# Token blocks of 512 with one u buffer, heads computed from row halves, first loads as two heads side by side

## The chip, the cores and the metric

One core of one Trainium2 chip runs the kernel. The metric is the device time of one execution in microseconds (us); a comparison uses the median of several runs.

## The reference

A batch of 8 sequences goes through attention and then through a feed-forward part. Cut to what matters:

```python
# q, k, v: (8 batches, 8 heads, 576 positions, 64); U (576, 32), V (32, 576)
# w_ch1 (512, 2048), w_ch2 (2048, 512)
scores = (q @ k.transpose(0, 1, 3, 2)) / 8
local   = (rel >= 0) & (rel < 32)                       # heads 0 to 3
strided = (rel >= 0) & (pos[None] % 32 == pos[:, None] % 32)   # heads 4 to 7
attn = softmax(np.where(mask, scores, -1e9))
x = (attn @ v).transpose(0, 2, 1, 3).reshape(8, 576, 512)
u = x + (x.transpose(0, 2, 1) @ U @ V).transpose(0, 2, 1)      # mixing over positions
out = u + np.maximum(u @ w_ch1, 0) @ w_ch2                     # on each token alone
```

U, V and both weight matrices arrive as 64-bit floats; the kernel makes each into two 32-bit parts, high and low.

## The kernel before

**Two halves of the work.** The feed-forward part is two chains of matmuls on TensorE. `gemm1(n, fc)` computes 128 of the 2048 hidden columns (`fc` from 0 to 15) for token block `n`: 12 matmuls into one PSUM bank `ph`, 4 slices of the 512 input columns times 3 products of high and low parts. ACT then makes `gh` (relu, rounded) and DVE makes `gl` (the rest). `gemm2` multiplies `gh` and `gl` with the second weights and adds into `acc`. A block has 256 tokens (two tiles of 128), so there are 18 blocks and 288 steps, each of 12 matmuls of 256 columns (`gemm1`, line 625) and 6 of 512 columns (`gemm2`, line 642). Blocks 0 and 1 are run interleaved (`NLEAD`), because the weights are still being converted then.

**Attention beside it.** Batches 0 and 1 (`attention_pair` with `early`) work on pairs of heads: TensorE transposes q and k (`transpose_natural`, line 203), ACT copies the result out in four pieces for each of q and k (lines 204 to 213), k into `kZ`, a buffer that holds the two heads on its diagonal and zeros elsewhere, so that one matmul of 128 rows does both heads (line 299, 18 of them, each in two passes). The strided heads of these batches use the same code on values that a DMA has reordered in DRAM (`sd`) and pass their result through DRAM (`od`). The local heads of batches 2 to 7 take q and k transposed by DVE (lines 287, 289); their strided heads (`strided_heads`) are products on GpSimd (lines 409, 437) and sums on DVE (lines 411, 439). `mix_t` and `mix_u` do the mixing over positions (lines 475, 479, 501, 508).

**The token transposes.** `transposes(n)` prepares `uh` and `ul`, the transposed block in two parts: on TensorE for three blocks (line 590), later by DVE and 16 DMAs. These live in a ring of 5 buffers with tag `u`, so the next block's parts can be written while this block's are read.

**What sets the order.** The Python loop at the end emits the steps of all of these side by side by a table of numbers at the top of the file; a scheduler then fixes the order of instructions on each engine, and each engine works in that order. Nearly all DMAs are issued by SP's queue. Weight chunks (32 of 512 KB) are loaded by line 157 and converted by `to_f32` and `weights` on ACT, DVE and GpSimd.

Of the kernel before, what the change touches and what calls it, by code (L numbers as in the profile page):

```python
# [7 lines left out]
F32 = mybir.dt.float32  # L8
# [9 lines left out]
ATT_BUFS = 7  # L18
NSP = 2
N_STEPS_1 = 90  # L20
N_LOCAL = 60
N_STRIDED = 66
LAG = 2
LAGB = 5
DUPS = 'aaaaaaaadapaaada'
EVK = 'aaaaaaaaaaaaaaaa'
EVQ = 'vaaaaaaaaaavaaaa'
PTS = 'vaaaaaaa'
CMODE = (1, 1, 1, 0, 1, 1, 1, 0)
W0, W1 = 2, 29  # L30
N_PE_T = 3
LD0, LDR = 4, 0.3
LDM = 4
CONVM = 1.35
NLEAD = 2
SKEW = 2
CLA = 2
SW0 = 2
SD_N = 1
S_END = 16  # L40
CONV0, CONV1, CONVE = 6, 99, 5
B1S, B1E = 24, 1
ORDER0, ORDER1 = (0, 2, 3, 1), (0, 2, 3, 1)
# [3 lines left out]
def fused_kernel(ctx, tc, q, k, v, U, V, w1_in, w2_in, masks, eye, out):  # L47
# [8 lines left out]
    FPG = NFC // NG  # L56

# [15 lines left out]
    def ubuf(shape, name, dtype=F32):  # L73
        return mp.tile(shape, dtype, name=name, tag="u", bufs=5)

    counts = {"xn": 0, "conv": 0}
    banks = {"n": 0, "prefix": True}

    def psx2():
        """Two PSUM banks; those of the output sums serve too before the first of them."""  # L80
        banks["n"] += 1
        if banks["prefix"] and banks["n"] % 3 == 0:
            return ps_acc.tile([128, 2, 512], F32, name="acc")
        return ps_x.tile([128, 2, 512], F32, name="px")
# [8 lines left out]
    def dma(out, in_):  # L93
        last_dma[0] = nc.sync.dma_start(out=out, in_=in_).ins  # L94

    ident = const.tile([128, 128], F32, name="ident")
    masks_sb = const.tile([128, 768], BF16, name="masks_sb")
    mask_b = masks_sb[:, 0:640].rearrange("p (a t x) -> p a t x", a=2, x=64)
    ident_b = masks_sb[:, 640:768]
    kZ = const.tile([128, 2, 32 + S], F32, name="kZ")  # L100
    nc.vector.memset(kZ, 0.0)
# [4 lines left out]
    def to_f32(raw, p, n, eng=nc.vector, one=False):  # L106
# [3 lines left out]
        cv = att([128, 512], "cv")  # L110
        f = cv[0:p, 0:n]
        if one:
            eng.tensor_scalar(out=f, in0=hi_w.bitcast(F32), scalar1=TINY, scalar2=None, op0=ALU.abs_max)
        else:
            nc.scalar.activation(out=f, in_=hi_w.bitcast(F32), func=AF.Abs)  # L115
# [669 lines left out]
```

## Time and profile before

| what | number |
|---|---|
| runs | 1017.5 us median, 1016.81 to 1020.14 |
| profiled execution: span from first to last instruction | 1016.9 us |
| TensorE matmul busy | 958.7 us (94%) |
| VectorE (DVE) busy | 648.8 us (64%) |
| ScalarE (ACT) busy | 313.0 us (31%) |
| GpSimd (POOL) busy | 406.1 us (40%) |
| first matmul of `gemm1` starts at | 90.94 us |

The profiled execution lies 0.6 us below the median of the runs. The page's chain of work that ended last puts 76% of the span on TensorE. The text calls the time before the first `gemm1` the opening, the time in which blocks 0 and 1 run the first 512 tokens.

### The profile page before, as it was taken

What the parts mean: (1) busy time and instruction counts of PE and PEld (TensorE: products, weight loads), DVE (VectorE), ACT (ScalarE), POOL (GpSimd) and SP (SyncE); (2) the same over time, 40 slices, a digit from 0 to 9 for tenths busy, and PEclk for the clock granted to TensorE, in tenths of its full rate; (3) what the DMA queues carried; (4) which work ended last, traced back from release to release, by engine and by line L of the source; (5) the groups of instructions that cost most, each with busy time, mean ns of one, the idle gap of its engine ahead of it and who ended that gap; (6) DMA issues with size and microseconds to landing.
All of it is one profiled execution on the core that took longest, in us unless ns stands there. A gap on an engine that the chain in (4) does not pass through costs nothing.

```text
span 1016.9 us, 18249 instructions
## 1 busy us (share of the span) xinstructions
PE 958.7 (94%) x7164; PEld 832.6 (82%) x7164; DVE 648.8 (64%) x1184; ACT 313.0 (31%) x691; POOL 406.1 (40%) x397
## 2 busy tenths in 40 slices
PE   4576889999999999999999999999999999999997
PEld 2345678898898889978889888988898889999996
DVE  3567998979786868634768686968686864312121
ACT  6777545213311241111422133123321242111110
POOL 1324966965383429201447353735383410000000
PEclk9797999999999999999999999999999999999999
DMA  7865913042523250401252425052514200101000
GB/s 189 221 164 143 366 39 67 2 109 48 91 42 68 48 90 22 88 1 42 47 91 43 68 47 91 21 89 48 91 39 71 47 22 21 42 1 43 1 21 21
DMA packets 186094, 71.33 MB, mean 70 GB/s; under 512 B 148952, under 2 KB 177272, under 8 KB 186008
## 3 DMA queue, kind: packets, MB, share of 16 engines
q1 hardware_dynamic: 186008, 70.16, 32.4%
q8 instruction: 56, 0.92, 0.4%
q14 instruction: 30, 0.25, 0.1%
HBM read 51.64 MB, written 11.80 MB: 62 GB/s over the span
## 4 chain that ended last, share of the span: by engine, by line
PE 76%; DVE 7%; SPq 5%; POOL 4%; issue 3%; DMA 3%; ACT 2%; DVEq 0%; POOLq 0%; ACTq 0%
PE ph L625 35%; PE acc L642 33%; SPq L94 4%; POOL tmp L409 3%; PE px L299 2%; PE px L340 1%; DVE cv L120 1%; DVE st L439 1%; PE px L330 1%; POOL w L170 1%; SPq L157 1%; DVE cv L122 1%; PE px L475 1%; DMA raw<-in_moe_w_ch_dram 1%; PE px L501 1%
## 5 line engine op out<-in xcount | busy, mean ns | idle before, releaser
L625 PE MATMUL ph<-uh,w 128*128 128x256 f32 x2304 | 472.6, 286 | 8.1 <-DVE gl L630 7.3
L625 PEld LDWEIGHTS ph<-uh,w 128*128 128x128 f32 x2304 | 379.3, 190 | 29.4 <-DVE gl L630 11.9
L642 PE MATMUL acc<-w,gh 128*128 128x512 f32 x1088 | 341.5, 393 | 0.0
L625 PE MATMUL ph<-ul,w 128*128 128x256 f32 x1152 | 331.5, 288 | 1.6 <-DVE ul L595 1.6
L630 DVE SCALAR_TENSOR_TENSOR gl<-ph,gh 128x256 fp32r<-128x256 f32 x288 | 120.6, 419 | 244.9 <-ACT gh L629 243.5
L629 ACT ACTIVATE gh<-ph 128x256 fp32r<-128x256 f32 x288 | 110.3, 384 | 504.9 <-PE ph L625 452.8
L437 POOL TENSOR_TENSOR tmp<-st,s_st 128x448 f32<-128x448 f32 (+7 forms) x162 | 144.2, 912 | 237.2 <-DVE st L439 148.7
L625 PEld LDWEIGHTS ph<-ul,w 128*128 128x128 f32 x1152 | 217.3, 189 | 11.4 <-DVE ul L595 1.8
L642 PEld LDWEIGHTS acc<-w,gh 128*128 128x128 f32 x1088 | 194.3, 188 | 31.2 <-issue 2.2
L642 PE MATMUL acc<-w,gl 128*128 128x512 f32 x544 | 213.2, 392 | 0.2 <-DVE gl L630 0.2
L409 POOL TENSOR_TENSOR tmp<-st 128x576 f32<-128x576 f32 (+6 forms) x162 | 169.4, 1089 | 74.9 <-DMA st<-in_k_dram 29.2
L439 DVE TENSOR_REDUCE st<-tmp 128x64 f32<-128x64 f32 (+8 forms) x162 | 138.3, 873 | 4.4 <-POOL tmp L437 3.4
L642 PEld LDWEIGHTS acc<-w,gl 128*128 128x128 f32 x544 | 102.2, 188 | 19.3 <-issue 1.1
L411 DVE TENSOR_REDUCE s_st<-tmp 128x9 f32<-128x576 f32 (+6 forms) x162 | 87.8, 564 | 14.2 <-POOL tmp L409 13.6
L170 POOL TENSOR_TENSOR w<-cv,w 128x512 fp32r<-128x512 f32 x32 | 45.3, 1424 | 49.1 <-ACT w L169 46.9
L116 POOL TENSOR_SCALAR cv<-cv 128x512 f32<-128x512 f32 x24 | 40.0, 1670 | 42.2 <-ACT cv L115 36.8
L454 ACT COPY xg<-st 32x256 f32<-32x256 f32 x96 | 38.7, 404 | 37.3 <-DVE st L439 36.4
L299 PE MATMUL px<-kZ,qT 128*32 128x128 f32 x612 | 30.5, 303 | 8.5 <-ACT qT L226 8.4
L299 PEld LDWEIGHTS px<-kZ,qT 128*32 128x32 f32 x612 | 20.4, 120 | 18.3 <-ACT qT L226 9.9
L169 ACT CAST w<-cv 128x512 fp32r<-128x512 f32 x32 | 19.7, 618 | 44.0 <-DVE cv L122 37.4
L612 DVE TENSOR_TENSOR ul<-u,uh 128x1024 fp32r<-128x1024 f32 x15 | 21.9, 1460 | 14.3 <-ACT uh L611 14.3
L120 DVE SCALAR_TENSOR_TENSOR cv<-raw,cv 128x512 int32<-128x512 int32 x32 | 28.3, 888 | 0.4
(123 smaller groups left out, 686.6 us busy)
## 6 DMA issues: line engine op xcount, KB each, us to landing
raw<-in_moe_w_ch_dram SPq DMA_DIRECT2D x32, 512.0 KB, 8.0
out_dram<-xg SPq DMA_DIRECT2D x32, 256.0 KB, 2.2
u<-bt SPq DMA_DIRECT2D x240, 32.0 KB, 1.9
vt_kept<-in_v_dram SPq DMA_DIRECT2D x28, 144.0 KB, 3.6
st<-in_q_dram SPq DMA_DIRECT2D x24, 144.0 KB, 3.4
st<-in_k_dram SPq DMA_DIRECT2D x24, 144.0 KB, 4.8
st<-in_v_dram SPq DMA_DIRECT2D x24, 144.0 KB, 3.2
xn<-in_k_dram SPq DMA_DIRECT2D x48, 72.0 KB, 2.4
```

The costliest lines, as they stand in the source:

```text
L94: last_dma[0] = nc.sync.dma_start(out=out, in_=in_).ins
L116: eng.tensor_scalar(out=f, in0=f, scalar1=TINY, scalar2=None, op0=ALU.max)
L170: nc.gpsimd.tensor_tensor(out=lo, in0=f, in1=hi.bitcast(F32), op=ALU.subtract)
L299: nc.tensor.matmul(sp[32 * c4:32 * c4 + 32, t], qT[:, 32 * c:32 * c + 32], kZ[:, :, 32 * c:32 * c + 64], start=not early, stop=True, skip_ ...
L409: nc.gpsimd.tensor_tensor(out=tmp[:, 0:n], in0=sk[:, j0:j0 + n], in1=sq[:, i:i + 1].broadcast_to([128, n, D]), op=ALU.mult)
L411: late.append(lambda tmp=tmp, n=n, i=i, j0=j0: nc.vector.tensor_reduce(out=s_st[:, i, j0:j0 + n], in_=tmp[:, 0:n], axis=AX.X, op=ALU.add))
L437: nc.gpsimd.tensor_tensor(out=tv, in0=sv[:, 0:i + 1, d0:d0 + step], in1=s_st[:, i, 0:i + 1].broadcast_to([128, i + 1, step]), op=ALU.mult)
L439: late.append(lambda tv=tv, i=i, d0=d0, step=step: nc.vector.tensor_reduce(out=o_st[:, i, d0:d0 + step], in_=tv.rearrange("p j d -> p d j" ...
L625: nc.tensor.matmul(ph[:, 0:W], w_parts[0, g, dc][:, part, fs], ut[:, :, :, dc, :], start=(dc == 0 and i == 0), stop=(dc == NDC - 1 and i = ...
L629: nc.scalar.activation(out=gh[:, 0:W], in_=ph[:, 0:W], func=AF.Relu)
L630: nc.vector.scalar_tensor_tensor(out=gl[:, 0:W], in0=ph[:, 0:W], scalar=0.0, in1=gh[:, 0:W].bitcast(F32), op0=ALU.max, op1=ALU.subtract)
L642: nc.tensor.matmul(accs[n][:, s, :], gt[:, cs], w_parts[1, g, f][:, part, :], start=(fc == 0 and i == 0), stop=(fc == NFC - 1 and i == 2))
```

## The change

**Blocks of 512 tokens.** A block is now four tiles of one batch (`blocks`), and a ninth block takes the last 64 positions of all batches. `gemm1` and `gemm2` each issue 12 matmuls of 512 columns, in 144 steps. `acc` takes four PSUM banks, and the banks of the attention go from two buffers of two to one (`ps_x`, `bufs=1`).

**One u buffer.** `transposes(n)` brings the transposed tokens to `raw`; `split(n)` makes the high and low part of all four tiles in the one buffer `u` when the last `gemm1` of the block before has been issued.

**Heads from row halves.** `kZ` goes away. q and k of two heads stand in rows 0 to 63 and 64 to 127 of one buffer, and `scores` and `outputs` issue 36 matmuls of 64 rows each instead of 18 of 128 rows; the two heads write to separate PSUM banks. The mask comes in by two matmuls with an identity in all batches (before, in batches 2 to 7, DVE added it).

**First loads.** `load_natural` loads each head by a DMA of 256-byte pieces (before, 512-byte pieces over both heads), so that one copy of 576 columns follows the transposes. The second copy of the values, which ACT made for most heads of batches 0 and 1, is a DMA (`values`). The first seven DMAs of batch 0 that are not k go to ACT's queue. Batch 1 starts after 10 steps of batch 0 instead of 24 (`B1S`), and a weight chunk is converted every 2 steps instead of every 5 (`CONVE`).

```diff
-    ps_acc = ctx.enter_context(tc.tile_pool(name="ps_acc", bufs=1, space=bass.MemoryType.PSUM))
+    ps_acc = ctx.enter_context(tc.tile_pool(name="ps_acc", bufs=2, space=bass.MemoryType.PSUM))
...
-    ps_x = ctx.enter_context(tc.tile_pool(name="ps_x", bufs=2, space=bass.MemoryType.PSUM))
+    ps_x = ctx.enter_context(tc.tile_pool(name="ps_x", bufs=1, space=bass.MemoryType.PSUM))
...
+    def values(vt, heads, eng=None):
+        for hh in range(2):
+            sv = heads[hh].rearrange("(c p) d -> p c d", p=32)
+            dma(out=vt[64 * hh + 32:64 * hh + 64, :, 0:D], in_=sv, eng=eng)
+            dma(out=vt[64 * hh:64 * hh + 32, 1:NCH, 0:D], in_=sv[:, 0:NCH - 1, :], eng=eng)
...
+    def scores(kT, qT, mask):
+        sp = psx2()
+        for hh in range(2):
+            nc.tensor.matmul(sp[:, hh, 0:320], ident_b, mask, start=True, stop=False, skip_group_check=True)
+        for c in range(NCH):
...
+            for hh, rows in enumerate(halves):
+                nc.tensor.matmul(sp[32 * c4:32 * c4 + 32, hh, x0:64 * t + 64], qT[rows, 32 * c:32 * c + 32],
+                                 kT[rows, k0:32 * c + 32], start=False, stop=True, skip_group_check=True,
+                                 tile_position=(64 * hh, 32 * c4))
...
+    def load_natural(src, h0, eng=None):
...
+        for hh in range(2):
+            dma(out=xn[:, 0:512].rearrange("p (t h d) -> p h t d", h=2, d=D)[:, hh],
+                in_=src[h0 + hh, 0:512].rearrange("(t p) d -> p t d", p=128), eng=eng)
...
+    blocks = [[(xg_b, t) for t in range(4)] for xg_b in range(B)] + [[("T", p) for p in range(B // 2)]]
...
+        uT[n] = mp.tile([128, 2, 4, 4, NDC, 32], F32R, name="u", tag="u", bufs=1)
...
+    def split(n):
+        u, raw = u_tile(n), raw_u[n]
+        for dc in range(NDC):
+            src, hi, lo = raw[:, :, :, dc, :], u[:, 0, :, :, dc, :], u[:, 1, :, :, dc, :]
+            nc.scalar.copy(out=hi, in_=src)
+            nc.vector.tensor_tensor(out=lo, in0=src, in1=hi.bitcast(F32), op=ALU.subtract)
...
-                nc.tensor.matmul(ph[:, 0:W], w_parts[0, g, dc][:, part, fs], ut[:, :, :, dc, :],
+                nc.tensor.matmul(ph, w_parts[0, g, dc][:, part, fs], uT[n][:, ut, :, :, dc, :],
                                  start=(dc == 0 and i == 0), stop=(dc == NDC - 1 and i == 2))
-        gh = mp.tile([128, 256], F32R, name="gh", bufs=3)
-        gl = mp.tile([128, 256], F32R, name="gl", bufs=3)
...
+        gh = mp.tile([128, 512], F32R, name="gh", bufs=2)
+        gl = mp.tile([128, 512], F32R, name="gl", bufs=2)
...
+                    if fc == NFC - 1 and n + 1 < NB:
+                        split(n + 1)
```

Three places show how the order moves. In the rows, `x12` is a count and the sizes are of what is written.

TensorE at a block change (the end of the eighth of 18 blocks before, of the fifth of 9 blocks after; `w_3_3` is the fourth slice of the last quarter of the weights, `w_0_0` the first of the first). Before, the new block's `gemm1` stands between the last `gemm2` of the old block:

```order
L625 MATMUL ph<-uh,w_3_3_1628 128x256
L642 MATMUL acc<-w_3_1_1695,gh 128x512 x2
L642 MATMUL acc<-w_3_1_1695,gl 128x512
L642 MATMUL acc<-w_3_1_1695,gh 128x512 x2
L642 MATMUL acc<-w_3_1_1695,gl 128x512
L625 MATMUL ph<-uh,w_0_0_257 128x256
```

After, ten more `gemm2` matmuls stand behind the old block's last `gemm1`, and then these rows up to the first step of the new block, which reads the new contents of the one buffer `u`:

```order
L604 MATMUL acc<-w_3_2_1785,gh 128x512 x2
L604 MATMUL acc<-w_3_2_1785,gl 128x512
L246 MATMUL px<-vt_84,PT_6177 32x65 x8
L604 MATMUL acc<-w_3_3_1794,gh 128x512 x4
L604 MATMUL acc<-w_3_3_1794,gl 128x512 x2
L246 MATMUL px<-vt_84,PT_6177 32x65 x28
L588 MATMUL ph<-u,w_0_0_231 128x512 x3
L588 MATMUL ph<-u,w_0_1_309 128x512 x3
L588 MATMUL ph<-u,w_0_2_386 128x512 x3
L588 MATMUL ph<-u,w_0_3_503 128x512 x3
```

So 18 `gemm2` matmuls and a head pair's 36 output matmuls stand between the last `gemm1` of the old block and the first of the new; a second step of `gemm1` (12 matmuls), 6 matmuls of `gemm2` and the third step of `gemm1` follow.

DVE at a block change. Before, the low part of the next block (line 612) is one instruction among the strided sums:

```order
L630 SCALAR_TENSOR_TENSOR gl<-ph,gh 128x256
L411 TENSOR_REDUCE s_st<-tmp 128x9
L612 TENSOR_TENSOR ul<-u,uh 128x1024
L411 TENSOR_REDUCE s_st<-tmp 128x7
L630 SCALAR_TENSOR_TENSOR gl<-ph,gh 128x256
```

After, between the last `gl` of a block (line 593) and the first of the next, with the four low parts of `split` (line 578) and the final sums of the old block (line 608):

```order
L593 SCALAR_TENSOR_TENSOR gl<-ph,gh 128x512
L436 TENSOR_REDUCE st<-tmp 128x32
L578 TENSOR_TENSOR u<-raw,u 128x16x32 x2
L436 TENSOR_REDUCE st<-tmp 128x32
L578 TENSOR_TENSOR u<-raw,u 128x16x32 x2
L436 TENSOR_REDUCE st<-tmp 128x32 x2
L608 TENSOR_TENSOR xg<-acc,xg 128x512 x2
L436 TENSOR_REDUCE st<-tmp 128x32
L256 TENSOR_SCALAR rt<-px 128x2x4
L436 TENSOR_REDUCE st<-tmp 128x32 x3
L257 RECIPROCAL rt<-rt 128x2x4
L593 SCALAR_TENSOR_TENSOR gl<-ph,gh 128x512
```

Eight sums, four low parts and two final sums of the old block now stand ahead of the new block's first `gl`.

ACT ahead of the first `gemm1`. Line 553 writes `u` for the four tiles of block 0; all four are needed by its first matmul. Three conversions, whose chunks are loaded after all of batch 1's q and k, stand between them:

```order
L553 CAST u<-acc 128x4x4x32
L227 ACTIVATE s_sb<-s_sb 128x640
L553 CAST u<-acc 128x4x4x32
L99 ACTIVATE cv<-raw_1_3_1150 128x512
L99 ACTIVATE cv<-raw_1_0_1228 128x512
L553 CAST u<-acc 128x4x4x32
L99 ACTIVATE cv<-raw_1_1_1245 128x512
L553 CAST u<-acc 128x4x4x32
```

Before, the same place has the two tiles of block 0 alone, with the first `gemm1` waiting for those two:

```order
L594 CAST uh<-px 128x4x4x32
L169 CAST w_0_2_789<-cv 128x512
L594 CAST uh<-px 128x4x4x32
```

The last write that the first `gemm1` needs now stands behind three more conversions, and so behind their loads.

More of the change, by code (lines that the diff above doesn't have):

```diff
@@ new lines, in fused_kernel, with x_tiles, copy @@
+    halves = [slice(64 * hh, 64 * hh + 64) for hh in range(2)]
+    held = {}
+    vts = []
+    def x_tiles(b):
+        if b not in xgs:
+            xgs[b] = xp.tile([128, 4, DM], F32, name="xg")
+        if b // 2 not in tails:
+            tails[b // 2] = tail("xt")
+        return xgs[b], tails[b // 2]
+    def copy(engine, out, in_):
+        if engine == "a":
+            nc.scalar.copy(out=out, in_=in_)
+        else:
+            (nc.vector if engine == "v" else nc.gpsimd).tensor_copy(out=out, in_=in_)
@@ new lines, in outputs @@
+    def outputs(PT, vt, p0):
+        op = psx2()
+        for c in range(NCH):
+            t, c4 = c // 4, c % 4
+            o4 = c4 + p0 // 32 if t == 4 else c4
+            for hh, rows in enumerate(halves):
+                nc.tensor.matmul(op[32 * o4:32 * o4 + 32, hh, (D + 1) * t:(D + 1) * t + D + 1], PT[rows, 32 * c:32 * c + 32],
+                                 vt[rows, c], start=True, stop=True, skip_group_check=True,
+                                 tile_position=(64 * hh, 32 * o4))
+        return op[:, :, 0:5 * (D + 1)].rearrange("p h (t x) -> p h t x", x=D + 1)
@@ L687, in fused_kernel @@
+    gen, sgen = second(1), None
+    for i, _ in enumerate(first(0)):
+        if i >= SW0:
+            next(sw, None)
+        if i >= CONV0 and i % CONVE == 0:
+            convert(counts["conv"] + 1)
+        if i >= B1S and i % B1E == 0:
+            next(gen, None)
+    u_tile(0)
+    for _ in transposes_pe(0):
+        convert(counts["conv"] + 1)
     banks["prefix"] = False
     pend = []
[L689 to L690 removed]
+    c0 = counts["conv"]
```

725 lines of the change are left out of this document (317 added, 408 removed).

## The prediction

> **What bounds the kernel now.** I read the page's slices of the span first, then the groups of instructions by shape, then the chain of waits. In the slices (busy tenths, 25 us each) TensorE is near full from about 150 us to the end, and only the first six slices leave it room:
>
> ```profile
> PE   4576889999999999999999999999999999999997
> DVE  3567998979786868634768686968686864312121
> PEclk9797999999999999999999999999999999999999
> ```
>
> Its two large groups are the feed-forward matmuls, and the chain says how fast they follow each other when nothing else is there (start, length, what):
>
> ```profile
> L625 PE MATMUL ph<-uh,w 128*128 128x256 f32 x2304 | 472.6, 286 | 8.1 <-DVE gl L630 7.3 <-ACT uh L594 0.7
> L642 PE MATMUL acc<-w,gh 128*128 128x512 f32 x1088 | 341.5, 393 | 0.0
> ...
> 879.44 2.91 PE ph L625 x24
> 882.35 3.17 PE acc L642 x14
> ...
> 924.45 2.91 PE ph L625 x24
> ```
>
> The means of 286 and 393 ns overlap; the pitch is what counts. It is 2.91/24 = 121.25 ns for 256 columns and 3.17/14 = 226.4 ns for 512. Sixteen steps of 12 and 6 make 45.0 us, just the distance from 879.44 to 924.45. All 288 steps cost 288 x (12 x 0.12125 + 6 x 0.2264) = 810.3 us of the 1016.9 us span. The same two lines counted by stretches of the span (busy, then count; line 625 first) give the rest:
>
> ```profile
> 90.90:205.60 114.70, 54.25 (x379) 50.83 (x380) 0.99 0.37 118
> 205.60:880.00 674.40, 348.06 (x2533) 332.68 (x2532) 1.00 0.32 57
> 880.00:1011.60 131.60, 73.08 (x548) 71.50 (x546) 1.00 0.06 19
> ...
> 90.90:205.60 114.70, 47.22 (x176) 30.70 (x176) 0.99 0.37 118
> 205.60:880.00 674.40, 327.15 (x1264) 223.66 (x1264) 1.00 0.32 57
> 880.00:1011.60 131.60, 72.30 (x288) 51.24 (x288) 1.00 0.06 19
> ```
>
> Counts times pitches: in the middle stretch (batches 2 to 7) 593 us are feed-forward and 81.3 us are not, 13.5 us for each batch. In the stretch of the first 512 tokens 85.8 us are feed-forward and 28.9 us are not. The last is pure. So the span is 90.9 (opening) + 114.7 + 674.4 + 131.6 + 5.3 (last sum and store). It lies 0.6 us under the median of the runs, and I add that at the end.
>
> **Part 1: wide gemm1.** The change turns 3456 matmuls of 256 columns into 1728 of 512. At the pitch that `gemm2` has with 512 columns of the same type, each pair saves 2 x 121.25 - 226.4 = 16.1 ns, 27.8 us in all. The bounds: the moving tokens of `gemm1` are read in runs of 32 elements and those of `gemm2` in one run, so at worst the pitch stays in proportion to columns and the gain is 0. I take 27.8: a fixed cost c and a cost per column from the two rows give c = 16 ns, and the 256-column rows are already read in such runs. Nothing can hide this gain, since TensorE is the engine that ends the chain. The Trainium skill, "TensorE: Matmul & The Clock Gate", section "Wait — 56ns, not 53.3ns?", puts the fixed cost of a matmul at about 2.5 ns; by that this part would be an estimated 1728 x 2.5 ns = 4.3 us. The trace does not agree: 226.4 and 121.25 ns stand where the page's sum gives 215.8 and 109.2.
>
> **Part 2: heads from row halves.** Before and after, per pair of heads (start, length of a merged run, what):
>
> ```profile
> 343.18 1.32 PE L340 MATMUL px<-vt_kept,PT 128*32 128x130 f32 x36
> 344.43 0.50 PE L642 MATMUL acc<-w,gl 128*128 128x512 f32 x1
> ...
> 349.70 1.28 PE L299 MATMUL px<-kZ,qT 128*32 128x128 f32 x36
> 350.92 0.43 PE L304 MATMUL px<-kZ,qT 128*64 128x128 f32 x2
> 351.28 0.39 PE L625 MATMUL ph<-uh,w 128*128 128x256 f32 x1
> ...
> 68.05 0.43 PE L479 MATMUL ph<-xt,U_sb 64*32 64x64 f32 x16
> ```
>
> ```profile
> L479 PE MATMUL ph<-xt,U_sb x16: 216/216/240, 68.0 to 68.3; 64*32 64x64 f32 x16
> ```
>
> Scores take 351.28 - 349.70 = 1.58 us, outputs 344.43 - 343.18 = 1.25 us. The shape that replaces them, 64 rows by 32 with 64 columns, is there in line 479: 16 records in 0.43 us, of which the last lasts 0.216, so 15 pitches of 14.3 ns. After, 72 records are 1.03 us. The two mask matmuls (640 columns) cost about 0.38 us, so scores are 1.41 and outputs 1.04: 0.38 less for each of 12 pairs, and 0.05 for a narrower transpose, -5.2 us. The bounds: as fast as that row, or 30 ns, the pitch of today's 128-column records without any gain for half the width (1.22 us / 36 = 34), which would add 22 us instead. I take the row of the same shape.
>
> **Part 3: the opening.** Here the path is a queue of loads, conversions and head pairs before the first `gemm1`:
>
> ```profile
> 90.94 0.50 PE L625 MATMUL ph<-uh,w 128*128 128x256 f32 x2 [0.68 <-ACT uh L594]
> ...
> 76.61 1.10 SPq L94 DMA_DIRECT2D xn<-in_q_dram  x2
> ...
> 46.10:49.00 2.90, 0.00 (x0) 0.00 (x0) 1.67 (x2) 2.83 (x7) 1.15 (x1) 0.69 0.72 216
> 268.00:272.00 4.00, 4.00 (x35) 3.06 (x28) 0.59 (x2) 0.72 (x3) 0.00 (x0) 1.00 1.36 170
> 98.00:108.00 10.00, 9.78 (x62) 8.40 (x62) 8.95 (x15) 6.99 (x15) 8.33 (x6) 0.98 0.95 352
> 0.00:90.90 90.90, 51.09 (x625) 35.86 (x625) 46.30 (x99) 67.32 (x108) 22.85 (x24) 0.85 0.73 184
> ```
>
> The last column is GB/s: 216 where q and k come in 512-byte pieces, 170 where everything comes in 256-byte pieces, 352 where weights come. ACT is the busiest engine of the opening (67.3 of 90.9 us). The change takes 13 copies of values and most of 64 part copies away there:
>
> ```profile
> L226 ACT COPY kZ<-acc 64x288 f32<-64x288 f32 x12 | 8.0, 664 | 1.4 <-PE acc L203 1.2
> L226 ACT COPY vt_kept<-vt_kept 32x1088 f32<-32x1088 f32 x6 | 6.7, 1112 | 0.1
> ```
>
> 13 x 1.11 = 14 us, and about 20 us of the 36 that the part copies take, so ACT no longer sets the pace. The loads do. From the order of SP's queue, ahead of batch 1's last q stand after the change 10.1 MB in 256-byte pieces, 1.5 MB in larger ones and 5.5 MB of weights, masks and U, V: 59.4 + 6.9 + 15.6 = 82 us, against 3.7, 6.0 and 5.5 MB, 22 + 28 + 16 = 65 us, before (where the last q is issued at 76.6 us, so 13 us more went in waits). Behind that q come values (0.6 MB), the `od` round trip and three weight chunks, about 15 us, and ACT's order sets those chunks' conversions ahead of the last write of `u`. With 5 us of waits the first `gemm1` starts at 102 us instead of 90.9: +11 us. Bounds: 87 us, if the conversions hold nothing up, and 115, if the loads wait as much as today.
>
> **Part 4: the first 512 tokens.** TensorE works there for 103.6 of 114.7 us:
>
> ```profile
> 90.90:205.60 114.70, 103.56 (x740) 88.76 (x741) 105.84 (x180) 50.05 (x101) 90.68 (x67) 0.99 0.37 118
> ```
>
> So 11.1 of the 28.9 us are idle and 17.8 are attention and transposes. By the order, after the change all eight pairs' scores and seven of eight outputs of batches 0 and 1 stand ahead of the first `gemm1`; of batch 1 only a transpose (0.65), an output (1.04), two `mix_t` (1.6), `mix_u` (1.15) and their switches (1.3) remain, 5.7 us. The 12 us that move into the opening lie beside its loads (TensorE works 51 of 90.9 us there). DVE, 105.8 of 114.7 us busy, is what TensorE idles for; 14 instead of 7 conversions are done before, so I leave 5 us of idle. 28.9 becomes 10.7: -18.2 us. Bounds: 8 to 22 us left.
>
> **Part 5: block changes.** Now `u` is single, and DVE must do, between the last `gl` of a block and the first of the next, what the excerpt of its order shows:
>
> ```profile
> L439 DVE TENSOR_REDUCE st<-tmp 128x32 f32<-128x576 f32 x12 | 14.2, 1203 | 0.0
> L439 DVE TENSOR_REDUCE st<-tmp 128x32 f32<-128x320 f32 x12 | 8.6, 727 | 0.0
> L649 DVE TENSOR_TENSOR xg<-acc,xg 128x512 f32<-128x512 f32 x30 | 19.4, 683 | 5.6 <-PE acc L642 5.3
> ...
> PE ph L625 <- DVE gl L630: 7.3, 8, 1.5
> ```
>
> Eight sums of about 1.0, six operations of 0.68 (line 649's shape), two small ones and the `gl` itself (0.68): 13.1 us, up to 1.3 less because neighbours overlap. TensorE waits for it at the third `gemm1` step, whose bank the first `gl` must free: 48 matmuls (10.9 us), the outputs (1.25) and switches, 12.5 us after the last `gemm1` of the old block. With relu in front (0.6) DVE is late by 0 to 1.2 us. I take 1 us for each of 8 changes, +8 us; bounds 0 and, if DVE comes late to it, 5 us each, 40 us. Behind this wait stands all of TensorE's queue. In the whole run today TensorE waits 7.3 us for `gl` before `gemm1`. The tail stays: one sum and the stores behind the last matmul.
>
> **Sum.** -27.8 - 5.2 + 11 - 18.2 + 8 = -32.2: 984.7 against the 1016.9 us of the profiled execution, 985 against the median.
>
> **Rivals.**
> - *The opening does not grow.* For it: ACT loses 34 us of work, seven first loads go to another queue. Against it: 10.1 MB at 170 GB/s. With the first `gemm1` at 87 us the time is 970.
> - *Small matmuls pay by record.* For it: today's 128-column records run at 34 ns, no row shows row halves by turns. Against it: 14.3 ns in line 479. At 25 ns, 24 sets of 72 records behind the opening cost 72 x 10.7 ns = 0.77 us each: +18.5, 1003 us. The Trainium skill, same page and section, states that start to start never drops below about 25 ns however small the matmul is; by that rule this would be the case, and the row of line 479 disagrees.
> - *The fixed cost of a matmul is not 16 ns but per column.* Against it: the two pitches. The gain of part 1 is then 0, 1012 us; by the page's 2.5 ns an estimated 1008.
> - *Slower: DVE is late at every block change.* Place: the third `gemm1` step of a block, waiting for the first `gl`. For it: 13.1 us of DVE work against 12.5 of cover, and the steps before it load DVE fully (sums and transposes). Against it: 64% DVE over the span. The sum without part 5 is 976.7, so it decides from 40.8/8 = 5.1 us per change; at 6 us it is 1025.
>
> **How the numbers follow.** The forecast has 0.55, with a range of its own of 968 to 1002; the opening that does not grow 0.20, records 0.11, columns 0.05, DVE late 0.09. The range takes the first three cases with the bounds of parts 3 to 5: 956 to 1012. The bound of a measurable difference is 0.3%, 3 us. All cases but the last are faster, the per-column one just about: faster 0.87, same 0.04, slower 0.09.
>
> **What the profile after would show.** Part 1: 24 matmuls of line 588 or 604 in a row at 226 ns each, 5.43 us a step. Part 2: a run of line 214 or 246 about 1.0 us long. Part 3: first line 588 at about 102 us, ACT's conversion waiting for weights before it. Part 4: first block ended about 98 us later. Part 5: line 588 waiting for `gl` of line 593 about 8 us in all, at eight places. Wrong would be: an opening over 115 us, `gemm1` at 240 ns, or a wait of several us at each change.

## The result and the profile after

The changed kernel takes 1045.3 us (median of 4 runs, 1042.2 to 1047.0) against 1018.1 for the kernel before: a ratio of 1.0262 with a 95% interval of 1.0237 to 1.0286. It is slower by 27 us where 32 us less were forecast, and lies outside the range of 956 to 1012. The profiled execution has a span of 1044.6 us.

The slices of the span (25 us each, busy tenths) show a longer opening at a low clock, and TensorE as the full engine behind it:

```profile
PE   4457798989999999989999999999999999999997
PEclk8566799999999999999999999999999999999999
```

The same three stages of both kernels, first after, then before, cut at the first `gemm1` and at the first `gemm1` of token 512. The columns are length; busy time and count of TensorE, its weight loads, DVE, ACT and POOL; granted clock; DMA share; GB/s:

```profile
0.00:110.49 110.49, 60.61 (x1265) 41.09 (x1265) 60.42 (x123) 46.56 (x74) 29.50 (x32) 0.68 0.94 203
110.49:223.13 112.64, 104.24 (x645) 78.56 (x646) 104.97 (x161) 39.35 (x69) 95.74 (x75) 0.95 0.43 113
223.13:1044.60 821.47, 792.89 (x4960) 614.09 (x4958) 445.24 (x734) 171.42 (x363) 274.98 (x290) 0.99 0.25 47
```

```profile
0.00:90.94 90.94, 51.09 (x625) 35.86 (x626) 46.34 (x99) 67.35 (x109) 22.89 (x24) 0.85 0.73 184
90.94:207.38 116.44, 105.34 (x750) 90.35 (x751) 107.50 (x182) 50.41 (x102) 92.42 (x69) 0.99 0.37 119
207.38:1016.90 809.52, 802.30 (x5790) 706.42 (x5788) 494.96 (x906) 195.22 (x481) 290.74 (x306) 1.00 0.28 50
```

So the opening is 19.6 us longer, the first 512 tokens are 3.8 us shorter, and the rest is 12.0 us longer. In the rest, TensorE is busy 9.4 us less, and stands still 28.6 us instead of 7.2.

The chain that ended last, in undisturbed steps near the end (start, length, what):

```profile
961.36 2.84 PE ph L588 x12
964.20 2.80 PE acc L604 x12
```

`gemm1` follows at 2.84/12 = 237 ns and `gemm2` at 2.80/12 = 233 ns. A step of 24 matmuls takes 5.645 us, where the same work took 2 x 2.813 = 5.63 us before and 5.43 was predicted. The first term of the sum is not there. (Pitches of single matmuls in this text, such as 226.8 ns for the kernel before, are means of the distances between starts in undisturbed steps near the end.)

What TensorE waited for (total, times, longest, in us):

```profile
PE ph L588 <- DVE gl L593: 14.2, 6, 3.0
...
PE ph L588 <- ACT u L553: 5.3, 1, 5.3
...
PE ph L588 <- DVE u L578: 4.2, 8, 0.6
```

A block change in the timeline of DVE, from the sums ahead of the old block's last `gl` on:

```profile
747.45 4.33 DVE L436 TENSOR_REDUCE st<-tmp 128x32 f32<-128x384 f32 x5
751.71 0.67 DVE L593 SCALAR_TENSOR_TENSOR gl<-ph,gh 128x512 fp32r<-128x512 f32 x1
752.31 0.99 DVE L436 TENSOR_REDUCE st<-tmp 128x32 f32<-128x480 f32 x1
753.24 2.25 DVE L578 TENSOR_TENSOR u<-raw,u 128x512 fp32r<-128x512 f32 x2
755.41 1.01 DVE L436 TENSOR_REDUCE st<-tmp 128x32 f32<-128x480 f32 x1
756.34 2.24 DVE L578 TENSOR_TENSOR u<-raw,u 128x512 fp32r<-128x512 f32 x2
758.50 2.02 DVE L436 TENSOR_REDUCE st<-tmp 128x32 f32<-128x512 f32 x2
760.45 1.27 DVE L608 TENSOR_TENSOR xg<-acc,xg 128x512 f32<-128x512 f32 x2
761.65 1.13 DVE L436 TENSOR_REDUCE st<-tmp 128x32 f32<-128x544 f32 x1
...
762.78 2.12 DVE L436 TENSOR_REDUCE st<-tmp 128x32 f32<-128x544 f32 x2
...
764.93 0.63 DVE L593 SCALAR_TENSOR_TENSOR gl<-ph,gh 128x512 fp32r<-128x512 f32 x1
```

The windows there (the 12.1 us ahead of the drop of the clock, their last 3.4 us, and the 3.4 us at half clock), and last a window at the block change at 223 us:

```profile
755.10:767.20 12.10, 9.49 (x42) 6.70 (x38) 12.10 (x17) 2.16 (x6) 2.69 (x2) 1.00 0.39 96
763.80:767.20 3.40, 1.58 (x7) 1.29 (x8) 3.40 (x7) 1.56 (x5) 0.00 (x0) 1.00 0.15 40
767.20:770.60 3.40, 3.40 (x10) 2.62 (x9) 1.47 (x5) 1.51 (x4) 0.00 (x0) 0.50 0.36 134
...
234.70:238.10 3.40, 1.71 (x7) 1.40 (x8) 3.40 (x6) 0.00 (x0) 2.91 (x4) 1.00 0.09 33
```

DVE works without a gap, sum after sum, up to the first `gl` of the new block at 764.93. TensorE idles 2.6 of the 12.1 us, and then the granted clock stands at 0.50 for 3.4 us. In it the feed-forward matmuls follow each other at 427 ns instead of 233 to 237: about eight of them, 1.5 us more. TensorE pauses at six of the eight block changes, and behind five of the pauses stands such a stretch. The Trainium skill, "TensorE: Matmul & The Clock Gate", section "What's actually happening", says that the array falls to half its clock after an idle window of about 3.4 us and comes back after a busy one of the same length; the rows agree on the length of the stretch. They do not agree on the idle window: in the 3.4 us just ahead of the five stretches TensorE was busy 0.74 to 1.58 us. At the change at 223 us the pauses fall so that no such window leaves it busy less than 1.71 us (last row), and the clock stays at 1.00.

### The profile page after: what moved, and what is told of

Read it like the earlier page. It is cut to its first block, busy times and chain, and to the rows that moved or that the text cites. A ratio compares the mean times of both kernels' runs of the same rounds, so it can differ in the third digit from the quotient of the medians.

```text
span 1044.6 us, 17173 instructions
## 1 busy us (share of the span) xinstructions
PE 957.7 (92%) x6868; PEld 733.8 (70%) x6868; DVE 610.6 (58%) x1015; ACT 257.3 (25%) x506; POOL 400.2 (38%) x396
## 4 chain that ended last, share of the span: by engine, by line
PE 53%; DVE 23%; DMA 8%; SPq 6%; POOL 3%; issue 3%; ACT 2%; ACTq 0%; DVEq 0%; POOLq 0%
PE ph L588 25%; PE acc L604 25%; DVE st L436 10%; SPq L84 6%; DMA raw<-in_moe_w_ch_dram 3%; DVE u L578 2%; DMA st<-in_v_dram 2%; DVE gl L593 2%; DVE cv L104 1%; DVE cv L106 1%; ACT xg L451 1%; POOL tmp L434 1%; DVE s_sb L224 1%; DVE mx L223 1%; POOL cv L100 1%
## 5 line engine op out<-in xcount | busy, mean ns | idle before, releaser
L588 PE MATMUL ph<-u,w 128*128 128x512 f32 x1728 | 455.9, 410 | 25.0 <-DVE gl L593 14.2
L588 PEld LDWEIGHTS ph<-u,w 128*128 128x128 f32 x1728 | 328.1, 192 | 117.1 <-DVE gl L593 16.5
L604 PE MATMUL acc<-w,gh 128*128 128x512 f32 x1152 | 361.6, 398 | 4.0 <-DVE xg L608 2.0
L604 PEld LDWEIGHTS acc<-w,gh 128*128 128x128 f32 x1152 | 216.7, 189 | 57.8 <-DVE xg L608 2.8
L593 DVE SCALAR_TENSOR_TENSOR gl<-ph,gh 128x512 fp32r<-128x512 f32 x144 | 98.8, 686 | 254.2 <-ACT gh L592 253.4
L592 ACT ACTIVATE gh<-ph 128x512 fp32r<-128x512 f32 x144 | 85.8, 596 | 458.6 <-PE ph L588 447.9
L408 DVE TENSOR_REDUCE s_st<-tmp 128x9 f32<-128x576 f32 (+6 forms) x162 | 86.9, 560 | 1.4 <-POOL tmp L406 0.8
L476 DVE TENSOR_TENSOR ta<-px,ta 32x256 f32<-32x256 f32 x42 | 17.6, 420 | 41.9 <-ACT ta L474 40.9
L102 DVE TENSOR_SCALAR cv<-cv 128x512 int32<-128x512 int32 (+3 forms) x35 | 22.4, 649 | 18.0 <-POOL cv L100 17.7
L578 DVE TENSOR_TENSOR u<-raw,u 128x512 fp32r<-128x512 f32 x32 | 30.8, 1004 | 0.0
L99 ACT ACTIVATE cv<-raw 128x512 f32<-128x512 f32 x32 | 21.4, 674 | 34.0 <-DMA raw<-in_moe_w_ch_dram 24.6
```

What stands on the lines that cost most here:

```text
L408: late.append(lambda tmp=tmp, n=n, i=i, j0=j0: nc.vector.tensor_reduce(out=s_st[:, i, j0:j0 + n], in_=tmp[:, 0:n], axis=AX.X, op=ALU.add))
L578: nc.vector.tensor_tensor(out=lo, in0=src, in1=hi.bitcast(F32), op=ALU.subtract)
L588: nc.tensor.matmul(ph, w_parts[0, g, dc][:, part, fs], uT[n][:, ut, :, :, dc, :], start=(dc == 0 and i == 0), stop=(dc == NDC - 1 and i == 2))
L592: nc.scalar.activation(out=gh, in_=ph, func=AF.Relu)
L593: nc.vector.scalar_tensor_tensor(out=gl, in0=ph, scalar=0.0, in1=gh.bitcast(F32), op0=ALU.max, op1=ALU.subtract)
L604: nc.tensor.matmul(acc, gt[:, cs], w_parts[1, g, f][:, part, :], start=(fc == 0 and i == 0), stop=(fc == NFC - 1 and i == 2))
```

## The experiments

All comparisons are against the kernel before, measured in the same session (1017.6 to 1020.0 us); experiments 1 to 5, 7, 8 and 13 start from the changed kernel.

**Why the wide `gemm1` gains nothing.** Four reasons were in question: the reading of tokens in runs of 32, a limit on the rate of TensorE, the data, and the places of the operands in memory.

Experiment 1: the token buffer in the order in which it is read.

```diff
-        uT[n] = mp.tile([128, 2, 4, 4, NDC, 32], F32R, ...)
+        uT[n] = mp.tile([128, 2, NDC, 4, 4, 32], F32R, ...)
-                nc.tensor.matmul(ph, w_parts[0, g, dc][:, part, fs], uT[n][:, ut, :, :, dc, :],
+                nc.tensor.matmul(ph, w_parts[0, g, dc][:, part, fs], uT[n][:, ut, dc].rearrange("p s a x -> p (s a x)"),
```

> The changed kernel with u stored so that the moving tokens of a gemm1 matmul are one run of 512 elements instead of 16 runs of 32. In the undisturbed steps of the changed kernel gemm1 matmuls follow each other at 237 ns and gemm2 matmuls at 232.5 ns, where 226.4 was predicted for both. Theory READ (the runs of 32 cost time): gemm1 falls to about 227 ns, gemm2 stays at 232.5, the time falls by 1728 x 10 ns = 17 us. Theory LIMIT (TensorE is held to about 0.459 ns per column whatever the cut of the work, the figure that the kernel before has as well: 5.627 us for 12288 columns): the sum of 24 matmuls stays at 5.645 us and the time within 3 us. Theory ADDRESS (the load of the next stationary tile and the moving stream hinder each other by where they lie): both pitches change, in either direction.

Measured: 1041.2 us, ratio 1.0218 (1.0194 to 1.0243). The chain, in steps near the end:

```profile
965.28 2.78 PE acc L604 x12
968.06 2.78 PE ph L588 x12
```

`gemm1` is now at 232 ns, just as `gemm2`. The runs cost 5 ns of the missing 10; something else holds both at 232.

Experiment 2: each `gemm1` matmul as two of 256 columns.

```diff
+                for h in range(2):
+                    nc.tensor.matmul(ph[:, 256 * h:256 * h + 256], w_parts[0, g, dc][:, part, fs],
+                                     uT[n][:, ut, 2 * h:2 * h + 2, :, dc, :], ...)
```

> The changed kernel with each gemm1 matmul of 512 columns issued as two of 256 into the two halves of the bank, each with its own load of the stationary tile. Theory LIMIT: the two pitches return to those before (121 and 227 ns), and a step of 24 x 512 columns stays at 5.63 us; the time stays within 3 us. Theory READ: two matmuls of 8 runs each cost 2 x 121 = 242.5 ns, gemm2 stays at 232.5: a step is 5.70 us, the time rises by 144 x 0.055 = 8 us. A fixed cost of 16 ns on each matmul with nothing else: gemm1 253 ns a pair, +28 us.

Measured: 1042.8 us, ratio 1.0248 (1.0228 to 1.0268).

```profile
965.26 2.80 PE acc L607 x12
968.06 2.88 PE ph L589 x24
```

A `gemm1` matmul of 256 takes 120 ns, and `gemm2` stays at 233 instead of returning to 227: a step is 5.68 us. LIMIT, which asked for 121 and 227, does not fit; READ's 5.70 does. The time did not rise by READ's 8 us: TensorE's pauses in the third stage, summed over the starts of its matmuls, fell from 22 to 18 us, and none of the five stretches of half clock is left there.

Experiment 3: zeros in `u`, `gh` and `gl` from the second block on, the instructions unchanged.

```diff
-            nc.scalar.copy(out=hi, in_=src)
-            nc.vector.tensor_tensor(out=lo, in0=src, in1=hi.bitcast(F32), op=ALU.subtract)
+            nc.scalar.activation(out=hi, in_=src, func=AF.Copy, scale=0.0)
+            nc.vector.tensor_tensor(out=lo, in0=src, in1=hi.bitcast(F32), op=ALU.mult)
...
-        nc.vector.scalar_tensor_tensor(out=gl, in0=ph, scalar=0.0, ..., op0=ALU.max, op1=ALU.subtract)
+        nc.vector.scalar_tensor_tensor(out=gl, in0=ph, scalar=0.0, ..., op0=ALU.mult, op1=ALU.subtract)
```

> The changed kernel with zeros in u from the second block on and in gl and gh with it (the feed-forward result is left out there); the same instructions in the same order. If the pitch depends on the data (a limit on the activity of the array), gemm1 and gemm2 fall to about 227 ns in blocks 2 to 9 and the time by 1536 x 10 + 1536 x 6 ns = 24 us. READ and ADDRESS: pitches of 237 and 232.5 ns stay, time within 5 us.

Measured: 1043.4 us in one run, and the chain shows the lengths of the changed kernel:

```profile
969.72 2.85 PE ph L588 x12
972.57 2.80 PE acc L604 x12
```

The data play no part in the pitches.

Experiments 5 and 6: an unused tile of 384 bytes ahead of `u`, `gh` and `gl`. In the compiled kernel before, the weights begin at byte 20384 of a partition, `uh` at 205728 and `gh` at 222112: 928 modulo 1024 for all. After the change the weights begin at 10208 (992), `u` at 192096 and `gh` at 216672 (608 for both), since the tiles in between have other sizes.

```diff
+    pad = ap_.tile([128, 96], F32, name="pad")
+    nc.gpsimd.memset(pad[:, 0:1], 0.0)
```

> The changed kernel with one unused tile of 384 bytes per partition ahead of u, gh and gl, so that these begin at the same place within 1024 bytes as the weights (992 for all four); in the kernel before they do (928 for all), in the changed kernel the weights begin at 992 and u, gh and gl at 608. Same instructions. Theory ADDRESS (the load of the next stationary tile and the moving stream hinder each other by where they lie): gemm2 returns from 232.5 to about 227 ns and gemm1 from 237 to about 232, 1728 x 10 ns = 17 us off the time. If the place plays no part, both pitches and the time stay within 3 us.

> The same shift of u, gh and gl by 384 bytes, with u stored so that a gemm1 matmul reads one run of 512 elements; that storage alone brought gemm1 from 237 to 232 ns and the time from 1045 to 1041. ADDRESS: both pitches at about 227 ns, 24 of them 5.43 us as predicted, and the time about 1041 - 3456 x 5 ns = 1024 us. If the place plays no part: 232 ns and 1041 us.

Measured: 1040.2 us (1.0205, 1.0178 to 1.0233) with the shift alone, 1031.3 us (1.0117, 1.0092 to 1.0142) with the shift and contiguous tokens. The chains of the two:

```profile
965.44 2.74 PE acc L604 x12
968.18 2.84 PE ph L588 x12
```

```profile
965.55 2.72 PE ph L588 x12
968.27 2.72 PE acc L604 x12
```

With the shift alone `gemm2` goes to 2.74/12 = 228 ns (by starts 226.7 from the sixth of the twelve on) and `gemm1`, still read in runs, stays at 237. With both, all 24 take 226.7 ns, and a step takes 2.72 + 2.72 = 5.44 us, what Part 1 said. So the gain of Part 1 was lost to two things that no row of the profile before could show together: tokens in 16 runs of 32 (10 ns with everything in place), and operands that no longer began at the same place.

The two could be one, since contiguous storage also moves the starts of the four token slices of a step: they lie 128 bytes apart in the changed kernel and 2048 in experiment 6. The trace of experiment 5 denies that. There the first slice begins at the weights' place, and its three matmuls take 235, 240 and 233 ns by starts, no less than the nine others.

The single operands begin in steps of 512 bytes within their buffers, so half of the pairs of experiment 6 lie 512 bytes apart modulo 1024, and they take 226 to 227 ns as well. So the place counts modulo 512 at most; and as 384 bytes matter, 128 and its divisors are out. No other shift was tried.

Experiment 6 is 14 us faster than the changed kernel, though the feed-forward of its third stage takes 22 us less (722.0 instead of 744.2, by starts): TensorE's pauses there grew from 22 to 30 us. The faster matmuls ran into the waits of the block changes.

Experiment 12: the opposite, the kernel before with the same pad.

> The kernel before with one unused tile of 384 bytes that moves uh, ul, gh and gl away from the place within 1024 bytes that they share with the weights; the same instructions. Theory ADDRESS: its pitches of 121 and 226.8 ns rise, gemm2 to about 232 ns and a pair of gemm1 matmuls by about 5, together up to 1728 x 10 = 17 us slower, about 1033. If the place plays no part here: 1018.

Measured: 1022.5 us, ratio 1.0038 (1.0024 to 1.0052).

```profile
965.50 1.44 PE ph L627 x12
966.94 1.87 PE acc L644 x8
```

`gemm2` rises from 226.8 to 1.87/8 = 234 ns, as ADDRESS has it, and the kernel is 5 us slower, not 17. `gemm1` of 256 columns does not rise (121.0 to 120.0), but for `gemm1` this run is no test: its four token slices begin 128 bytes apart, so before and after the shift alike one of the four begins at the weights' place modulo 512, and three do not. The place is shown to matter in both kernels for `gemm2`, and for `gemm1` by experiments 1 and 6.

Experiment 14: the kernel of experiment 6 with each `gemm1` matmul as two of 256 columns.

> The kernel with contiguous, shifted u (24 matmuls of 512 columns at 226.7 ns, 1031 us), with each gemm1 matmul issued as two of 256 columns. Theory FIXED (the prediction's: about 13 to 16 ns for each matmul besides its columns): a gemm1 matmul of 256 takes 120 to 121 ns, a pair 13 to 16 ns more than one of 512, and the time rises by 1728 x 14 ns = 24 us. Theory RUNS (the 121 ns of the kernel before came from reading tokens in runs of 32, not from a fixed cost): 113.5 ns, a pair as long as one of 512, and the time stays within 3 us.

Measured: 1040.1 us, ratio 1.0216 (1.0192 to 1.0239).

```profile
965.20 2.75 PE acc L607 x12
967.95 2.87 PE ph L589 x24
```

2.87/24 = 120 ns: FIXED holds against RUNS' 113.5. With tokens contiguous and in place, 512 columns take 226.7 and 256 take 120 ns, which on a straight line is 0.417 ns per column and 13.3 ns for each matmul. Two points do not test a line, but the same trace has a third and a fourth, in a stretch of half clock (758.5 to 761.9 us):

```profile
759.66 0.43 PE ph L589 x2
760.09 1.28 PE acc L607 x3
```

By starts, 256 columns take 213 ns there and 512 take 427: 0.834 ns per column, twice 0.417, and nothing for each matmul. So the 13.3 ns are there at full clock and not at half. The same holds for the runs and the places: in the stretches of half clock of the changed kernel and of experiments 1, 5 and 6, 512 columns take 427 ns in all four.

The kernel lost 9 us to experiment 6 and not 24: in the third stage the feed-forward grew by 20 us, and TensorE's pauses fell from 30 to 20 us. That slower matmuls gave DVE time is the likely reading, as experiment 6 shows the opposite. The Trainium skill, "TensorE: Matmul & The Clock Gate", section "Wait — 56ns, not 53.3ns?", has about 2.5 ns for the fixed cost; the trace differs also here.

**The block changes.** Experiment 4: the strided sums earlier.

```diff
-N_STRIDED, SS, SE = 64, -9, 2
+N_STRIDED, SS, SE = 64, -15, -7
```

> The changed kernel with the strided sums spread over steps -15 to -7 of the block change instead of -9 to 2, so that from the third block change on no sum stands on DVE between the last gl of the old block and the first of the new. In the changed kernel TensorE idles 3.0 to 4.8 us at each of the six block changes in the middle and its granted clock then stands at half for 3.4 us. Theory LATE-DVE (the single u buffer makes TensorE wait for DVE's queue, and the pause costs half the clock for 3.4 us): the pauses at changes 3 to 7 fall to under 1 us, the clock stays at full, and the time falls by 4 x (3.3 + 1.7) = 20 us or somewhat less. Rival (the four splits alone hold TensorE up, whatever stands between them): pauses stay over 2 us and the time falls by less than 8 us.

Measured: 1078.7 us, ratio 1.0596 (1.0577 to 1.0616). The waits from 330 us on, largest and the one of the block changes:

```profile
PE acc L604 <- DVE gl L593: 17.5, 15, 2.6
...
PE ph L588 <- ACT u L577: 0.8, 1, 0.8
```

The pauses at the changes were gone, and so was the half clock from 380 us on. But the sums, crowded into eight steps, made `gemm2` wait for `gl` there. Blocks 3 to 5 gained 0.8 to 1.6 us each, and blocks 6 to 9 nothing. The wait was moved, not removed. The time was lost in the second block, which is 149.7 us long: it holds 45 of the sums of line 436 instead of 37, TensorE pauses 26.8 us in it instead of 4.8, and the granted clock is 0.90. Which of these began it stays open.

Experiment 9: on the kernel of experiment 6, the sums of batches 3 to 7 over 14 steps that end before the change, those of batch 2 as they were.

```diff
+                    ss, se = (SS, SE) if sb == NSP else (-15, -1)
-                    a, z = NFC * (sb - 1) + SS, NFC * (sb - 1) + SE
+                    a, z = NFC * (sb - 1) + ss, NFC * (sb - 1) + se
```

> The kernel with contiguous, shifted u (1031 us) with the strided sums of batches 3 to 7 spread over steps -15 to -1 of the block change instead of -9 to 2, so that at the changes from the third on only the four splits, two to four final sums and two other instructions stand on DVE between the gl of the two blocks. Theory LATE-DVE: the pauses at these changes (3 to 5 us each, and half the clock for 3.4 us behind four of them) end, and as the sums are not crowded into eight steps as in the earlier trial, no gemm2 waits for gl instead: time about 1031 - 5 x 4 = 1011. Rival SPLIT (the four splits by themselves hold TensorE up): under 6 us gained.

Measured: 1002.8 us, ratio 0.9852 (0.982 to 0.9884), 28.5 us less than experiment 6. The largest wait of TensorE from 330 us on is

```profile
PE acc L604 <- DVE gl L593: 0.9, 1, 0.9
```

against 12.5 us for `gl` and 6.9 for `u` in experiment 6, and no stretch of half clock follows a block change behind 345 us. TensorE's pauses in the third stage fell from 30.0 to 8.8 us. LATE-DVE holds: the four splits fit under TensorE's work, the sums beside them did not.

**The opening.** Experiment 7: 1-KB pieces for q and k.

```diff
-            dma(out=xn[:, 0:512].rearrange("p (t h d) -> p h t d", h=2, d=D)[:, hh],
-                in_=src[h0 + hh, 0:512].rearrange("(t p) d -> p t d", p=128), eng=eng)
+            dma(out=xn[:, 256 * hh:256 * hh + 256],
+                in_=src[h0 + hh, 0:512].rearrange("(p t) d -> p (t d)", t=4), eng=eng)
```

> The changed kernel with q and k of batches 0 and 1 loaded in pieces of 1 KB instead of 256 bytes (same bytes, same number of transfers; positions come jumbled, so the heads of these two batches are left wrong). In the changed kernel the first gemm1 starts at 110.5 us. Theory PIECES (the opening is limited by small pieces): 8 MB at 170 GB/s are 47 us and at 350 GB/s 23 us, so the first gemm1 starts 10 to 20 us earlier. Rival QUEUE (SP's order and the waits in it, od's way through DRAM and the conversions that stand ahead of the last write of u): under 4 us earlier.

Measured: the first `gemm1` starts at 109.7 us, 0.8 earlier; 1050.2 us in one run. The size of the pieces does not limit the opening, though Part 3 built its 59 us of loads on it. Nor does the clock: in this run it stood at 0.95 over the opening, against 0.68 in the changed kernel.

Experiment 8: the two numbers of the opening as before.

```diff
-CONV0, CONVE = 4, 2
-B1S, B1E = 10, 1
+CONV0, CONVE = 4, 5
+B1S, B1E = 24, 1
```

> The changed kernel with the two numbers of the opening as before: batch 1 starts after 24 steps of batch 0 instead of 10, and a chunk is converted every 5 steps instead of every 2. Only 8 of the 16 score sets' mask matmuls' pairs then stand ahead of the first gemm1. Theory MOVED (what left the opening comes back in the first block): first gemm1 near 75 us, the first 512 tokens take as much longer, and the time stays within 10 us of 1045. Theory FREED (TensorE's stalls in the opening are saved): the end of the first 512 tokens comes 10 us or more earlier than 223 us.

Measured: 1088.6 us, ratio 1.0692 (1.0656 to 1.0727).

```profile
0.00:87.21 87.21, 37.45 (x702) 24.79 (x702) 42.57 (x91) 31.64 (x52) 20.34 (x24) 0.78 0.84 193
87.21:265.90 178.69, 137.45 (x1141) 98.40 (x1141) 119.42 (x190) 54.46 (x90) 98.92 (x76) 0.80 0.42 105
```

The first `gemm1` comes 23 us earlier and the first 512 tokens end 43 us later. Both theories fall. Behind the first `gemm1` TensorE waits 41 us, of which 15 us are for converted weights (lines 159 and 160), and the clock is at 0.80. The heads of batch 1 and the later conversions came into this stage together, so the run does not tell which of the two numbers costs the time.

Experiment 10: on experiment 6, the conversions, all but one, behind the last write of `u` in ACT's order. ACT in the changed kernel, and then in the experiment:

```profile
108.00 0.66 ACT L99 ACTIVATE cv<-raw 128x512 f32<-128x512 f32 x1 [1.80 <-DMA raw<-in_moe_w_ch_dram]
108.56 0.57 ACT L553 CAST u<-acc 128x512 fp32r<-128x512 f32 x1
```

```profile
104.19 0.66 ACT L100 ACTIVATE cv<-raw 128x512 f32<-128x512 f32 x1 [3.25 <-DMA raw<-in_moe_w_ch_dram]
104.76 1.06 ACT L558 CAST u<-acc 128x512 fp32r<-128x512 f32 x2
```

```diff
-        convert(counts["conv"] + 1)
+        pass
...
-        nc.scalar.activation(out=f, in_=hi_w.bitcast(F32), func=AF.Abs)
+            with tc.issue_after(u_last[0]):
+                nc.scalar.activation(out=f, in_=hi_w.bitcast(F32), func=AF.Abs)
```

> The kernel with contiguous, shifted u with the weight conversions of the last four opening steps set behind the last write of u on ACT. In the changed kernel that write waited behind three conversions whose chunks SP issued at 100.85 us, and TensorE stood still for 5.3 us ahead of the first gemm1 at 110.5 us. Theory GATE: the first gemm1 starts at about 105 us, and the time falls by up to 5 us; rival: the first steps then wait for the later conversions, the end of the first 512 tokens stays at 223 us and the time within 2 us of 1031.

Measured: 1029.3 us, ratio 1.011 (1.0086 to 1.0134). The first `gemm1` starts at 105.9 instead of 109.5 us, and the first 512 tokens end at 223.4 instead of 223.0: the rival's case. What is gained ahead of the first matmul is waited for behind it.

Experiment 11: experiments 9 and 10 together.

> Both changes together. If they are independent, the sum of both gains: 1031 - 20 - 5 = 1006 us, faster than before (1018) by about 1 per cent. If they hit the same bound (DVE), less than the sum.

Measured: 1001.5 us (1000.6 to 1003.6), ratio 0.984 (0.9816 to 0.9864), the fastest version and faster than both kernels.

```profile
0.00:107.39 107.39, 59.08 (x1264) 40.15 (x1264) 58.56 (x118) 45.36 (x73) 28.51 (x32) 0.71 0.92 196
107.39:224.30 116.91, 102.39 (x646) 78.00 (x646) 109.45 (x166) 40.58 (x71) 99.57 (x78) 0.96 0.44 121
224.30:1000.20 775.90, 761.45 (x4960) 609.39 (x4958) 446.05 (x733) 171.12 (x363) 268.95 (x289) 1.00 0.27 50
```

Against the kernel before, the third stage is 33.6 us shorter, and the first two together 16.9 us longer. The gate adds 1.4 us to experiment 9's gain, within what its interval can tell.

**The first 512 tokens.** Experiment 13: without the strided work of batch 2, which lies in this stage.

```diff
-            for j0 in range(0, i + 1, 9):
+            for j0 in range(0, i + 1 if b != NSP or not i else 0, 9):
...
-            for d0 in range(0, D, step):
+            for d0 in range(0, D if b != NSP or not i else 0, step):
```

> The changed kernel without the strided products and sums of batch 2 (only the first row of each is made, the strided heads of that batch are left wrong). In the changed kernel they take 41 us of POOL and 21 us of DVE in the stage of the first 512 tokens (110.5 to 223.1 us), where DVE is busy 104.9 of 112.6 us, POOL 95.7 and TensorE idles 8.4 us and runs 14 us at half its clock. Theory DVE (with POOL beside it, DVE is what that stage takes, not TensorE, and it did not get less work by the change): the stage falls by 8 us or more, to 104 or less. Rival (TensorE's 90 us of feed-forward at its pitch, its attention and the half clock set it): it falls by less than 4 us. The third block's stage may fall too, since the sums at its block change go away.

Measured: 1030.8 us, ratio 1.011 (1.0081 to 1.0139).

```profile
109.97:221.46 111.49, 104.31 (x720) 78.60 (x721) 86.69 (x134) 42.10 (x78) 56.20 (x39) 0.97 0.47 115
221.46:321.88 100.42, 99.95 (x721) 77.11 (x719) 62.07 (x109) 23.46 (x47) 49.59 (x53) 1.00 0.35 63
```

DVE lost 18 us of work in the stage and POOL 40, and the stage lost 1.1: theory DVE falls. The 14 us come from the next blocks instead, the second alone 6.4 us (106.85 to 100.42), where TensorE now idles 0.5 us instead of 4.8. The stage of the first 512 tokens is TensorE's own work, with its waits and a clock below full, and what orders those waits beyond the conversions stays open.

## Why the prediction was wrong

- **Part 1, the step that failed most.** "I take 27.8" took the pitch of `gemm2`'s 512 columns for `gemm1` too. The mechanism was right: the fixed cost is there at full clock, 13.3 ns by experiment 14 against 16 in the text. But a pitch was carried over as if it belonged to a shape. `gemm1` took 237 ns, and even `gemm2`, whose instructions did not change, went from 226.8 to 233. By step lengths, 144 x 5.645 - 288 x 2.813 = +2.7 us stood where -27.8 was written. A wide `gemm1` matmul did take 5 ns less than the two narrow ones (8 us in all), but `gemm2` lost 11 us. The lower bound, "the gain is 0", was named for the runs of 32; the place of the operands was not thought of. Experiment 6 shows the 226.7 ns. It also shows that "Nothing can hide this gain" was wrong: of the 22 us by which the feed-forward of its third stage is shorter than in the changed kernel, 8 went into longer pauses.
- **Part 2, right in kind, small in size.** The shape runs as its row said. Scores and outputs in the changed kernel:

```profile
637.66 0.92 PE L214 MATMUL px<-xT 64*32 64x32 f32 x72
...
754.33 0.84 PE L246 MATMUL px<-vt,PT 64*32 64x65 f32 x56
```

  0.92 us for 72 records is 10 to 13 ns each, so the rival of 25 ns a record falls. Summed over the starts of all matmuls in the third stage, scores, outputs and their transposes take 31.9 us instead of 43.9: -12, where -5.2 was taken.
- **Part 3, mis-sized.** +11 taken, +19.6 measured; still inside its bounds (115). The conversions did hold the last write of `u` (5.3 us of wait, "5 us of waits" in the text), but the loads' time was derived from piece size, and experiment 7 denies that. The last q left SP's queue at 88.6 us instead of 82, behind waits of the queue. Experiment 10 takes out the wait for the conversions and leaves the end of the first 512 tokens where it was. What sets the length of the opening stays open.
- **Part 4, wrong.** 98 us taken, 112.6 measured. By the starts of all matmuls, 96.1 us are feed-forward (86.9 taken: 3.4 us of the difference are Part 1's pitch, the rest the clock, 0.95 over the stage), 7.5 attention and mixing (5.7 taken) and 8.4 idle (5 taken). The text left the clock out altogether: after a stretch of waits TensorE ran at half speed from 108.4 to 118.6 us.
- **Part 5, right place, wrong size.** The place, the third `gemm1` step waiting for the first `gl`, is what the chain of waits shows, and the 13.1 us of DVE work measured 13.2 (from the start of one `gl` at 751.71 to that of the next at 764.93). That agreement is partly luck: at this change there are seven sums, not eight, and the low parts took 1.12 us each where 0.68 was written. Two things were missing in the 1 us per change: the old block's last `gl` itself started 1.3 us after its `gh` was there, behind five sums, and five of the six pauses were followed by 3.4 us of half clock. TensorE idled 2.6 to 4.8 us in each of the six blocks that begin with such a change, 21.8 us in all, and lost another 1.5 us behind five of the changes. Experiments 9 and 13 show that the sums are the cause: without those of batch 2, the pauses of the second block fall from 4.8 to 0.5 us.
- **The rivals.** The one that ended slower had the right mechanism, but its price stayed under the 5.1 us from which it alone would decide. The per-column rival had the right effect (no gain from Part 1) for a reason that experiment 14 refutes. No single rival came true: Parts 1, 3, 4 and 5 all came out slower than written, and only Part 2 faster.

## What to carry to other kernels

A pitch read from a trace belongs to the operands as they lie, not to the shape of the matmul alone: where a change alters buffer sizes, compare the start addresses of the stationary and the moving operand, and store the moving one in the order in which it is read. A buffer that is left single moves work of another engine into one place; what else stands on that engine there must be cleared away, by spreading it over the whole block and not by crowding it into a smaller part. Where the pauses at a block change left TensorE busy for less than half of a stretch of 3.4 us, half clock followed in the changed kernel: add its 1.5 us to the price of such a pause.

## What the runs showed of the hardware

- At full clock the pitch of a 512-column matmul of this type is 226.7 ns when the buffers of the stationary and the moving operand begin at the same place modulo 512 bytes and the moving one is contiguous, 232 ns when one is shifted by 384 bytes, and 237 ns when the moving one is read in runs of 32, shifted or not. Zeros instead of data change nothing. At half clock it is 427 ns in all these cases.
- A fixed cost of 13.3 ns for each matmul shows at full clock (120 ns for 256 columns, 226.7 for 512) and none at half clock (213 and 427).
- `gemm2` in place needs a few matmuls to settle behind some neighbours: in experiments 5 and 14 the first five of twelve take 228 to 236 ns and the others 227; in the kernel before, behind 256 columns read in runs, all but the first take 226.7.
- At the block changes of the changed kernel, 3.4 us of half clock followed windows of 3.4 us in which TensorE was busy 0.74 to 1.58 us. A window in which it was busy 1.71 us was not followed by it.
- Matmuls of 64 rows by 32 that alternate between the two halves of the rows follow each other at 10 to 13 ns.
